# Converting the first 16 weight pieces in pairs (128x1024 operations)

## The chip, the cores and the metric

The kernel runs on one core of one Trainium2 chip. The core has five engines that work side by side, each through its own queue in order: TensorE (PE, matmuls; its weight loads are shown as PEld), VectorE (DVE), ScalarE (ACT), GpSimd (POOL) and SyncE (SP, which here issues most DMAs). The metric is the time of one execution in device microseconds (us). Before the change the median of three runs is 1157.33 us (1157.27 to 1157.82).

## The reference

```python
x = attention(q, k, v)              # 4 batches, 8 heads, 768 positions, 64 each; window 128, 4 sink columns
x = x.transpose(0, 2, 1, 3).reshape(3072, 512)
h = np.maximum(x @ w_in, 0.0)       # w_in (512, 2048)
x = h * h @ w_out                   # w_out (2048, 512), both in float64
e = argmax(x @ w_gate)              # 8 experts, one per token
out = gate_w * eom * (np.maximum(x @ w1[e], 0) @ w2[e])
```

Attention goes into a dense layer pair (w_in, w_out), and that into a layer pair of one expert per token. w_in and w_out arrive as float64. [...]

## The kernel before, in words

The 3072 tokens are 12 blocks (t) of 256. A block goes through attention, in four head pairs (p) of two 128-row pieces, into `xr`; `split_x(t)` then writes `xT`, a high part on ACT and a low part on DVE, in four column groups kk (lines 542 and 543). The dense pair of a block is 16 steps (j): `l1(t, j)` is 12 matmuls of 256 columns (line 576) over the four kk, then a relu on ACT (line 579), a square on DVE or, for odd j of block 0, on POOL (line 580), and the split into high and low `h` (lines 582, 583); `l2(t, j)` is 6 matmuls of 512 columns (line 592). While block t goes through the dense pair, the attention of block t+1 is threaded between its matmuls. The expert stage follows.

The weights are made ready only once, during attention of block 0 and the dense steps of block 0. A *piece* is a slice of w_in (even numbers c) or of w_out (odd c); step j needs pieces 2j and 2j+1, and there are 32. `conv(c)` issues the load of a piece (512 KB) and returns `rest`, which converts it: two ACT operations on the raw words (lines 293, 296), two DVE operations that join the bits in `fbuf` (lines 298, 299), an ACT operation for the high part (line 300) and a DVE operation for the low part (line 301), all 128x512. That is 96 ACT and 96 DVE operations for 32 pieces. `fetch` issues loads two pieces ahead of `cstep`, which converts. Raw pieces lie in three `braw` buffers (the first three) and then in three rotating `stage` buffers; `fbuf` has two halves.

The order of the instructions on each engine is fixed when the program is built: a list scheduler takes, engine by engine, the ready instruction with the highest priority, mostly the earliest in the source. 13 pieces are converted, in source order, ahead of `split_x(0)`, 4 more at step j=0, then two per step. What is ready when, as the scheduler sees it, decides what stands ahead of what. On the chip every engine then follows that list and waits in place.

`xT` has one buffer, so block 1 can be split only when the last `l1` of block 0 has read it. The accumulators of `l1` (`psH`) are two.

Of the kernel before, what the change touches and what calls it, by code (L numbers as in the profile page):

```python
# [8 lines left out]
F32 = mybir.dt.float32  # L9
F32R = mybir.dt.float32r  # L10
BF16 = mybir.dt.bfloat16
I32 = mybir.dt.int32
U32 = mybir.dt.uint32
AF = mybir.ActivationFunctionType
ALU = mybir.AluOpType
# [10 lines left out]
NF = DFF // 128  # L26
# [9 lines left out]

SPLITS = {6: (0, 0), 8: (2, 0), 11: (0, 1), 12: (1, 0), 13: (2, 1), 14: (3, 0)}

NBOOT = 3
NSLOT = NT // 128 + NE - 1  # L40
PRE = 2

# [2 lines left out]
def kern(ctx, tc, q, k, v, n_sink, window, w_in, w_out, w_gate, w_og, w1, w2, out):  # L45
    nc = tc.nc
    V, A, G, PE, SY = nc.vector, nc.scalar, nc.gpsimd, nc.tensor, nc.sync
# [203 lines left out]
    cv = ctx.enter_context(tc.tile_pool(name="cv", bufs=1, side="right"))  # L251
# [15 lines left out]
    WO = [wpool.tile([128, NF // 2, 2, 512], F32R, name="WOa"), None]  # L267
    WIf = WI[:].rearrange("p j a k f -> p (j a k f)")
    WOf = [WO[0][:].rearrange("p j a f -> p (j a f)"), None]

    fbuf = att.tile([128, 2, 512], F32, tag="PT", name="fbuf", bufs=1)

    def conv(c):
        j, which = divmod(c, 2)
        if c < NBOOT:
            raw, dq = braw[c], A
        else:
            raw = cv.tile([128, 512, 2], I32, tag="stage", bufs=3, name="craw")
            dq = SY
        if which == 0:  # L280
            x = dq.dma_start(out=raw[:].rearrange("p (k f) w -> p k (f w)", k=4),
                         in_=w_in.bitcast(I32)[:, 256 * j:256 * j + 256].rearrange("(k p) f -> p k f", p=128))
            hi, lo = (WI[:, j, n].rearrange("p k f -> p (k f)") for n in range(2))
        else:
            x = dq.dma_start(out=raw[:].rearrange("p f w -> p (f w)"), in_=w_out.bitcast(I32)[128 * j:128 * j + 128, :])
            hi, lo = (WO[j // 8][:, j % 8, n] for n in range(2))
        if c < NBOOT:
            tc.keep_in_program_order(x)

        def rest():  # L290
            L, Hh = raw[:, :, 0], raw[:, :, 1]

            x = A.activation(out=Hh.bitcast(F32), in_=Hh.bitcast(F32), func=AF.Copy, scale=2.0 ** -112)
            if c < NBOOT:
                tc.keep_in_program_order(x)
            A.activation(out=L, in_=L.bitcast(U32), func=AF.Copy, scale=0.93 * 2.0 ** -29)
            f, fi = fbuf[:, c % 2], fbuf[:, c % 2].bitcast(I32)
            V.scalar_tensor_tensor(out=fi, in0=Hh, scalar=3, in1=L, op0=ALU.logical_shift_left, op1=ALU.bitwise_or)
            V.scalar_tensor_tensor(out=fi, in0=Hh, scalar=-2147483648, in1=fi, op0=ALU.bitwise_and, op1=ALU.bitwise_or)
            A.activation(out=hi, in_=f, func=AF.Copy)  # L300
            V.tensor_tensor(out=lo, in0=f, in1=hi.bitcast(F32), op=ALU.subtract)
        return rest
# [473 lines left out]
    NC = 2 * NF  # L776
    rests = {}
    st_ = dict(load=0, done=0)

    def fetch(n):  # L780
        while st_["load"] < n:
            rests[st_["load"]] = conv(st_["load"])
            st_["load"] += 1

    def cstep(n):
        for _ in range(n):
            if st_["done"] >= NC:
                return
            fetch(min(NC, st_["done"] + 2))
            rests.pop(st_["done"])()  # L790
            st_["done"] += 1

# [8 lines left out]
            general(gp_)  # L801
    bootS = ExitStack()
    boot = bootS.enter_context(tc.tile_pool(name="boot", bufs=1))
    braw = [boot.tile([128, 512, 2], I32, name=f"braw{n}") for n in range(NBOOT)]
    fetch(NBOOT)
    events = sorted((e for t in range(NBLK) for e in attn_events(t)), key=lambda e: e[0])
    events.reverse()

    def run_to(h):
        while events and events[-1][0] <= h:  # L810
            h_, f = events.pop()
            with (tc.high_priority(200) if h_ < 0 else ExitStack()):
                f()
# [8 lines left out]
    for h in range(-46, 0):  # L822
        run_to(h)
        if h == -38:
            setup2()
        if h >= -39 and h % 3 == 0:
            cstep(1)
    bootS.close()
    wpool2 = ctx.enter_context(tc.tile_pool(name="wpool2", bufs=1))
    WO[1] = wpool2.tile([128, NF // 2, 2, 512], F32R, name="WOb")  # L830
    WOf[1] = WO[1][:].rearrange("p j a f -> p (j a f)")
    split_x(0)

    raw = None

    def load_raw(pc, e, reg=False):

        o = raw[pc]
        if pc < 2:
            a_ = w1[bass.ds(e, 1)] if reg else w1[e:e + 1]  # L840
            SY.dma_start(out=o[:], in_=a_.rearrange("o (k p) f -> p (o k) f", p=128)[:, :, 512 * pc:512 * pc + 512])
        else:
            a_ = w2[bass.ds(e, 1)] if reg else w2[e:e + 1]
            SY.dma_start(out=o[:], in_=a_.rearrange("o (k p) f -> p (o k) f", p=128)[:, 4 * (pc - 2):4 * (pc - 2) + 4, :])
# [103 lines left out]
    for g in range(G2):  # L948
        t, j = divmod(g, NF)
        if t == NBLK - 2 and j == 8:  # L950
            presel()
        if t == NBLK - 1 and j == 0:
            run_to(2 * g - 0.1)
            attS.close()
            m2 = ctx.enter_context(tc.tile_pool(name="m2", bufs=1))
            raw = [m2.tile([128, 4, 512], F32, name=f"raw{pc}") for pc in range(4)]
            pidx = m2.tile([128, NSLOT], I32, name="pidx")
            xgr = [m2.tile([128, XW], F32, name=f"xg{n}")[:] for n in range(PRE)]
            es = [nc.values_load(pre[0:1, n:n + 1], engines=[ET.SP], min_val=0, max_val=NE - 1) for n in range(3)]
            for pc in range(4):  # L960
                load_raw(pc, es[0], True)
            box["base"] = nc.values_load(pre[0:1, 3:4], engines=[ET.SP], min_val=0, max_val=(NE - 1) * REG)
            for s in range(PRE):
                places(s)
                gather(s)
        if t == NBLK - 1 and j in SPLITS:
            pc, half = SPLITS[j]
            split_raw(pc, 4096 * half, True)
            load_raw(pc, es[half + 1], True)
        if t == 0:  # L970
            cstep(max(2 * j + 3, 17 + j) - st_["done"])
        with (tc.high_priority(20) if t == 0 else ExitStack()):
            swap = t > 0 and j == 0
            if swap:
                l2(*divmod(g - 2, NF))
            else:
                l1(t, j)
            run_to(2 * g + 0.9)
            if j == NF - 1 and t + 1 < NBLK:
                split_x(t + 1)  # L980
            if swap:
                l1(t, j)
            elif g >= 2:
                l2(*divmod(g - 2, NF))
            if g >= 2:
                if j == 1 and t > 0:
                    gate_events(t - 1)
            run_to(2 * g + 1.9)
# [149 lines left out]
```

## Time and profile before

| | |
|---|---|
| median of three runs | 1157.33 us |
| the profiled execution | 1156.13 us |
| its span, first to last instruction | 1154.4 us |
| PE, DVE, ACT, POOL busy | 97%, 63%, 56%, 36% |
| mean granted TensorE clock | 0.991 |
| conversion operations, first to last start | 22.8 to 129.5 us |

From about 135 us on PE is busy nearly all the time. The stage of the change is the first 135 us; there DVE and ACT are the busier engines. Each digit of the page's slices is the busy share of 28.9 us, too coarse for this stage, so the rows below are taken from finer views.

### The profile page before, as it was taken

How to read it: one execution, taken by the hardware profiler on the slowest of the kernel's cores; microseconds unless marked ns; L12 is line 12 of the kernel's file. 1: busy time of each engine (PE TensorE's matmuls, PEld its weight loads, DVE VectorE, ACT ScalarE, POOL GpSimd, SP SyncE). 2: the span in 40 equal slices, each digit the busy share in tenths (PEclk: the TensorE clock that was granted, in tenths of full speed). 3: DMA queues.
4: the chain of work that ended last, by engine and by line, in shares of the span. 5: the costliest groups of instructions: out<-in, count | busy, mean ns of one | idle time of the engine just before them, and what ended most of it. 6: DMA issues, size and time to landing. Idle time of an engine off the chain costs nothing. (4 is left out here: it accounts for less than half of the span.)

```text
span 1154.4 us, 23899 instructions
## 1 busy us (share of the span) xinstructions
PE 1118.4 (97%) x7082; PEld 943.0 (82%) x7082; DVE 731.2 (63%) x2039; ACT 642.0 (56%) x1761; POOL 418.4 (36%) x915
## 2 busy tenths in 40 slices
PE   8979999999999999999999999999999999999996
PEld 4657788888888888888888888997788888888884
DVE  4898867676767667676667676567312576763153
ACT  4988776767677767677767676453222222222200
POOL 3123463355564336565326665210211231111111
PEclk8989999999999999999999999999999999999998
DMA  6666211111211111211112110394411455753110
GB/s 156 186 207 182 72 28 50 39 50 37 54 28 49 38 46 36 56 29 43 35 47 47 38 31 1 63 224 153 129 47 46 167 190 191 241 195 119 48 44 24
DMA packets 139611, 100.08 MB, mean 87 GB/s; under 512 B 104127, under 2 KB 112447, under 8 KB 139458
## 3 DMA queue, kind: packets, MB, share of 16 engines
q1 hardware_dynamic: 131618, 82.28, 25.8%
q0 software_dynamic: 5408, 14.19, 3.8%
q10 hardware_dynamic: 2432, 1.84, 0.5%
q8 instruction: 64, 1.05, 0.4%
q14 instruction: 89, 0.73, 0.3%
HBM read 85.56 MB, written 13.76 MB: 86 GB/s over the span
## 5 line engine op out<-in xcount | busy, mean ns | idle before, releaser
L576 PE MATMUL psh<-xT,WI 128*128 128x256 f32 x2304 | 311.6, 284 | 4.2 <-ACT WI L300 2.1
L576 PEld LDWEIGHTS psh<-xT,WI 128*128 128x128 f32 x2304 | 293.6, 189 | 19.6 <-ACT WI L300 3.1
L906 PE MATMUL psh<-WI,xt 128*128 (+1 forms) x672 | 165.1, 399 | 1.0 <-ACT xt L886 0.7
L592 PE MATMUL psx<-WOa,h 128*128 128x512 f32 x576 | 159.0, 410 | 5.2 <-ACT h L582 4.7
L580 DVE TENSOR_TENSOR r<-r 128x256 f32<-128x256 f32 x184 | 85.5, 465 | 116.3 <-ACT r L579 115.2
L592 PE MATMUL psx<-WOb,h 128*128 128x512 f32 x576 | 155.3, 406 | 1.9 <-ACT h L582 1.6
L906 PEld LDWEIGHTS psh<-WI,xt 128*128 128x128 f32 x672 | 123.9, 188 | 29.3 <-ACT xt L886 1.4
L592 PEld LDWEIGHTS psx<-WOa,h 128*128 128x128 f32 x576 | 101.8, 190 | 23.4 <-ACT h L582 5.5
L592 PEld LDWEIGHTS psx<-WOb,h 128*128 128x128 f32 x576 | 101.4, 188 | 21.9 <-ACT h L582 2.9
L439 ACT ACTIVATE P<-P,st 128x260 f32<-128x260 f32 (+1 forms) x192 | 93.8, 489 | 44.5 <-DVE st L436 35.3
L922 DVE TENSOR_TENSOR ht<-psht,ht 128x512 fp32r<-128x512 f32 x56 | 38.5, 689 | 125.1 <-ACT ht L886 124.7
L579 ACT ACTIVATE r<-psh 128x256 f32<-128x256 f32 x192 | 71.7, 373 | 61.6 <-PE psh L576 58.8
L484 POOL TENSOR_SCALAR_AFFINE_SELECT PT<-PT 128x256 fp32r<-128x256 f32 x224 | 98.3, 472 | 17.1 <-DVE PT L480 16.9
L944 POOL DMA_INDIRECT out_dram<-xg,pidx x28 | 30.9, 1103 | 202.4 <-ACT xg L943 160.8
L583 DVE TENSOR_TENSOR h<-r,h 128x256 fp32r<-128x256 f32 x192 | 87.1, 454 | 18.2 <-ACT h L582 12.9
L582 ACT ACTIVATE h<-r 128x256 fp32r<-128x256 f32 x192 | 79.2, 414 | 27.6 <-DVE r L580 23.2
L436 DVE CUSTOM_DVE_ANT_0 P<-pss,M 128x260 f32<-128x260 f32 (+1 forms) x184 | 72.6, 403 | 20.1 <-PE pss L432 9.7
L935 PE MATMUL psy<-WOb,ht 128*128 (+1 forms) x336 | 85.1, 402 | 0.0
L912 ACT ACTIVATE r<-psh 128x512 f32<-128x512 f32 x48 | 28.7, 598 | 101.0 <-PE psh L906 99.1
L935 PE MATMUL psy<-WOa,ht 128*128 (+1 forms) x336 | 84.0, 397 | 0.0
L451 ACT ACTIVATE P<-P,st 128x132 f32<-128x132 f32 (+2 forms) x168 | 62.2, 415 | 34.2 <-DVE st L442 34.1
L935 PEld LDWEIGHTS psy<-WOa,ht 128*128 128x128 f32 x336 | 62.7, 188 | 14.7
(440 smaller groups left out, 1854.9 us busy)
## 6 DMA issues: line engine op xcount, KB each, us to landing
raw<-in_moe_w_dram SPq DMA_DIRECT2D x36, 1024.0 KB, 5.7
craw<-in_moe_w_out_dram SPq DMA_DIRECT2D x15, 512.0 KB, 3.5
craw<-in_moe_w_in_dram SPq DMA_DIRECT2D x14, 512.0 KB, 3.8
x2tab<-x2s SPq DMA_DIRECT2D x24, 256.5 KB, 3.0
kn<-in_k_dram SPq DMA_DIRECT2D x64, 96.0 KB, 2.5
vn<-in_v_dram SPq DMA_DIRECT2D x64, 96.0 KB, 2.2
qn<-in_q_dram SPq DMA_DIRECT2D x92, 64.0 KB, 2.1
kn<-in_k_dram SPq DMA_DIRECT2D x32, 64.0 KB, 1.9
```

Source lines behind the costliest of these rows:

```text
L436: V.tensor_tensor_reduce(out=P[:, e, 0:W], in0=ps[e][:, 0:W], in1=mask[:, 0:W], scale=-SCALE, scalar=3.0e38, op0=ALU.add, op1=ALU.min, acc ...
L439: A.activation(out=P[:, e, 0:W], in_=P[:, e, 0:W], func=AF.Exp, scale=-1.0, bias=st[:, e:e + 1], accum_out=st[:, 4 + e:5 + e])
L451: A.activation(out=P[:, e, 0:W], in_=P[:, e, 0:W], func=AF.Copy, scale=st[:, 6 + e:7 + e])
L484: G.affine_select(out=both[:, 1 - b, e], in_=bf[:, 0, e], pattern=[[0, 2], [1 - 2 * b, 128]], compare_op=ALU.is_gt if b else ALU.is_ge, fi ...
L576: PE.matmul(ps[:], lhsT=WI[:, j, a_, kk, :], rhs=x[:, b_, kk, :], start=(n == 0), stop=(n == 11))
L579: A.activation(out=hq[:], in_=ps[:], func=AF.Relu)
L580: (G if t == 0 and j % 2 else V).tensor_tensor(out=hq[:], in0=hq[:], in1=hq[:], op=ALU.mult)
L582: A.activation(out=o[:, 0], in_=hq[:], func=AF.Copy)
L583: V.tensor_tensor(out=o[:, 1], in0=hq[:], in1=o[:, 0].bitcast(F32), op=ALU.subtract)
L592: PE.matmul(acc[t][m][:], lhsT=o[:, a_, 128 * m:128 * m + 128], rhs=WO[j // 8][:, j % 8, b_, :], start=(j == 0 and n == 0), stop=(j == NF ...
L906: PE.matmul(ps[:], lhsT=o[:, a_, kk, :], rhs=wview(n, par + 2048 * b_ + 512 * kk, 512), start=(c == 0), stop=(c == 11))
L935: PE.matmul(yp[s][:], lhsT=o[:, a_, kk, :], rhs=wview(2 + n, par + 2048 * b_ + 512 * kk, 512), start=(n == 0 and kk == 0 and c == 0), stop ...
```

## The change

For the first 16 pieces (8 pairs: step j's slice of w_in and of w_out) the two raw pieces lie side by side in one `braw` buffer, and the first two ACT and the first two DVE operations of the conversion run once on both, 128x1024, into a `bf` buffer of two slices. The high and the low part stay 128x512 per piece. There are three `braw` buffers of a pair (8 KB per partition each) and two `bf` (4 KB each). These 32 KB are where the last eight slices of the second weights (`WOb`) are put later, so `WOb` is made at step j=0 and not ahead of `split_x(0)`. Loads run up to three pairs ahead (`fetch`) where they ran two pieces ahead; the first four are issued by ACT, the others by SP. Pieces 16 to 31 are converted as before.

```diff
--- before.py
+++ after.py
@@ -36,7 +36,7 @@
 
 SPLITS = {6: (0, 0), 8: (2, 0), 11: (0, 1), 12: (1, 0), 13: (2, 1), 14: (3, 0)}
 
-NBOOT = 3
+NBOOT = 16
 NSLOT = NT // 128 + NE - 1
 PRE = 2
 
@@ -273,30 +273,39 @@
     def conv(c):
         j, which = divmod(c, 2)
         if c < NBOOT:
-            raw, dq = braw[c], A
+            if which == 0:
+                braw[j] = boot.tile([128, 2, 512, 2], I32, tag="pair", bufs=3, name="braw")
+            raw, dq = braw[j][:, which], A if c < 4 else SY
         else:
-            raw = cv.tile([128, 512, 2], I32, tag="stage", bufs=3, name="craw")
+            raw = cv.tile([128, 512, 2], I32, tag="stage", bufs=3, name="craw")[:]
             dq = SY
         if which == 0:
-            x = dq.dma_start(out=raw[:].rearrange("p (k f) w -> p k (f w)", k=4),
+            x = dq.dma_start(out=raw.rearrange("p (k f) w -> p k (f w)", k=4),
                          in_=w_in.bitcast(I32)[:, 256 * j:256 * j + 256].rearrange("(k p) f -> p k f", p=128))
             hi, lo = (WI[:, j, n].rearrange("p k f -> p (k f)") for n in range(2))
         else:
-            x = dq.dma_start(out=raw[:].rearrange("p f w -> p (f w)"), in_=w_out.bitcast(I32)[128 * j:128 * j + 128, :])
+            x = dq.dma_start(out=raw.rearrange("p f w -> p (f w)"), in_=w_out.bitcast(I32)[128 * j:128 * j + 128, :])
             hi, lo = (WO[j // 8][:, j % 8, n] for n in range(2))
-        if c < NBOOT:
+        if c < 4:
             tc.keep_in_program_order(x)
 
         def rest():
-            L, Hh = raw[:, :, 0], raw[:, :, 1]
-
-            x = A.activation(out=Hh.bitcast(F32), in_=Hh.bitcast(F32), func=AF.Copy, scale=2.0 ** -112)
-            if c < NBOOT:
-                tc.keep_in_program_order(x)
-            A.activation(out=L, in_=L.bitcast(U32), func=AF.Copy, scale=0.93 * 2.0 ** -29)
-            f, fi = fbuf[:, c % 2], fbuf[:, c % 2].bitcast(I32)
-            V.scalar_tensor_tensor(out=fi, in0=Hh, scalar=3, in1=L, op0=ALU.logical_shift_left, op1=ALU.bitwise_or)
-            V.scalar_tensor_tensor(out=fi, in0=Hh, scalar=-2147483648, in1=fi, op0=ALU.bitwise_and, op1=ALU.bitwise_or)
+            if c < NBOOT and which == 0:
+                src = braw[j][:].rearrange("p c f w -> p (c f) w")
+                bf[j] = boot.tile([128, 2, 512], F32, tag="bf", bufs=2, name="bf")
+                f_ = bf[j][:].rearrange("p c f -> p (c f)")
+            elif c >= NBOOT:
+                src, f_ = raw, fbuf[:, c % 2]
+            if c >= NBOOT or which == 0:
+                L, Hh, fi = src[:, :, 0], src[:, :, 1], f_.bitcast(I32)
+
+                x = A.activation(out=Hh.bitcast(F32), in_=Hh.bitcast(F32), func=AF.Copy, scale=2.0 ** -112)
+                if c < 4:
+                    tc.keep_in_program_order(x)
+                A.activation(out=L, in_=L.bitcast(U32), func=AF.Copy, scale=0.93 * 2.0 ** -29)
+                V.scalar_tensor_tensor(out=fi, in0=Hh, scalar=3, in1=L, op0=ALU.logical_shift_left, op1=ALU.bitwise_or)
+                V.scalar_tensor_tensor(out=fi, in0=Hh, scalar=-2147483648, in1=fi, op0=ALU.bitwise_and, op1=ALU.bitwise_or)
+            f = bf[j][:, which] if c < NBOOT else f_
             A.activation(out=hi, in_=f, func=AF.Copy)
             V.tensor_tensor(out=lo, in0=f, in1=hi.bitcast(F32), op=ALU.subtract)
         return rest
@@ -786,7 +795,8 @@
         for _ in range(n):
             if st_["done"] >= NC:
                 return
-            fetch(min(NC, st_["done"] + 2))
+            n = st_["done"]
+            fetch(min(NC, max(n + 2, min(NBOOT, n // 2 * 2 + 6))))
             rests.pop(st_["done"])()
             st_["done"] += 1
 
@@ -801,8 +811,8 @@
             general(gp_)
     bootS = ExitStack()
     boot = bootS.enter_context(tc.tile_pool(name="boot", bufs=1))
-    braw = [boot.tile([128, 512, 2], I32, name=f"braw{n}") for n in range(NBOOT)]
-    fetch(NBOOT)
+    braw, bf = {}, {}
+    fetch(4)
     events = sorted((e for t in range(NBLK) for e in attn_events(t)), key=lambda e: e[0])
     events.reverse()
 
@@ -825,10 +835,6 @@
             setup2()
         if h >= -39 and h % 3 == 0:
             cstep(1)
-    bootS.close()
-    wpool2 = ctx.enter_context(tc.tile_pool(name="wpool2", bufs=1))
-    WO[1] = wpool2.tile([128, NF // 2, 2, 512], F32R, name="WOb")
-    WOf[1] = WO[1][:].rearrange("p j a f -> p (j a f)")
     split_x(0)
 
     raw = None
@@ -967,6 +973,12 @@
             pc, half = SPLITS[j]
             split_raw(pc, 4096 * half, True)
             load_raw(pc, es[half + 1], True)
+        if g == 0:
+            cstep(NBOOT - st_["done"])
+            bootS.close()
+            wpool2 = ctx.enter_context(tc.tile_pool(name="wpool2", bufs=1))
+            WO[1] = wpool2.tile([128, NF // 2, 2, 512], F32R, name="WOb")
+            WOf[1] = WO[1][:].rearrange("p j a f -> p (j a f)")
         if t == 0:
             cstep(max(2 * j + 3, 17 + j) - st_["done"])
         with (tc.high_priority(20) if t == 0 else ExitStack()):
```

The change moves instructions on every engine until some way into block 1; from there on the lists are the same. Two places matter here (line numbers of the changed kernel are 9 to 12 higher: 552 is 543, 306 and 307 are 298 and 299, 310 is 301, 585 is 576, 349 is 340, 477 is 468, 511 is 502).

On DVE, around the low parts of `xT` for block 0. Before the change:

```order
L449 TENSOR_SCALAR P<-P,st 128x260 x2
L298 SCALAR_TENSOR_TENSOR fbuf<-craw 128x512
L301 TENSOR_TENSOR WOa<-fbuf,WOa 128x512
L299 SCALAR_TENSOR_TENSOR fbuf<-craw,fbuf 128x512
L298 SCALAR_TENSOR_TENSOR fbuf<-craw 128x512
L543 TENSOR_TENSOR xT<-xr,xT 128x256
L299 SCALAR_TENSOR_TENSOR fbuf<-craw,fbuf 128x512
L301 TENSOR_TENSOR WI<-fbuf,WI 128x512
L543 TENSOR_TENSOR xT<-xr,xT 128x256
L301 TENSOR_TENSOR WOa<-fbuf,WOa 128x512
L543 TENSOR_TENSOR xT<-xr,xT 128x256 x2
```

On the same engine, after the change, the last part of the same stretch:

```order
L307 SCALAR_TENSOR_TENSOR bf<-braw,bf 128x1024
L552 TENSOR_TENSOR xT<-xr,xT 128x256 x3
L306 SCALAR_TENSOR_TENSOR bf<-braw 128x1024
L310 TENSOR_TENSOR WI<-bf,WI 128x512
L310 TENSOR_TENSOR WOa<-bf,WOa 128x512
L307 SCALAR_TENSOR_TENSOR bf<-braw,bf 128x1024
L306 SCALAR_TENSOR_TENSOR bf<-braw 128x1024
L310 TENSOR_TENSOR WI<-bf,WI 128x512
L310 TENSOR_TENSOR WOa<-bf,WOa 128x512
L307 SCALAR_TENSOR_TENSOR bf<-braw,bf 128x1024
L552 TENSOR_TENSOR xT<-xr,xT 128x256
```

Counted from the start of the list, 18 conversion operations of 512 columns stood ahead of the fourth low part of `xT`; now 14 of 1024 and 12 of 512 do. Ahead of the first square (line 580) it was 21 of 512, and is 15 of 1024 and 16 of 512. Ahead of the first relu on ACT (line 579) it was 22 of 512, and is 16 of 1024 and 19 of 512. Ahead of the first low part of `xT` for block 1 it was 96, and is 16 of 1024 and 64 of 512, which is all of them.

On PE, at the start of the dense steps of block 0. Before:

```order
L468 MATMUL pspt<-ident,P 128x128 x4
L576 MATMUL psh<-xT,WI 128x256 x8
L340 MATMUL psk__1291<-ident,kn 128x128 x3
L502 MATMUL pso<-PT_1262,vn 64x128 x2
L576 MATMUL psh<-xT,WI 128x256 x6
L502 MATMUL pso<-PT_1262,vn 64x128 x2
L576 MATMUL psh<-xT,WI 128x256 x10
```

After, with `psk` and `pso` of block 1's attention as above:

```order
L477 MATMUL pspt<-ident,P 128x128 x4
L585 MATMUL psh<-xT,WI 128x256 x35
L349 MATMUL psk__1259<-ident,kn 128x128
L585 MATMUL psh<-xT,WI 128x256 x2
L349 MATMUL psk__1259<-ident,kn 128x128
L585 MATMUL psh<-xT,WI 128x256 x4
```

The attention of block 1 stood between the first `l1` matmuls; now nearly three whole steps stand in one run, with nothing of block 1 between.

## Rows read from the trace of the kernel before

**Rows 1.** Stretches: us, busy of PE, PEld, DVE, ACT, POOL (instructions), clock, DMA share, GB/s.
```profile
26.00:47.00 21.00, 18.77 (x122) 11.20 (x121) 18.57 (x58) 19.43 (x55) 4.69 (x18) 1.00 0.59 149
53.00:130.00 77.00, 65.52 (x384) 50.59 (x383) 70.56 (x159) 65.35 (x152) 23.03 (x42) 0.96 0.63 185
...
130.00:140.00 10.00, 9.89 (x67) 8.17 (x66) 7.99 (x29) 8.36 (x29) 3.77 (x14) 1.00 0.06 15
140.00:150.00 10.00, 9.01 (x65) 7.72 (x64) 6.86 (x20) 7.20 (x21) 8.23 (x21) 1.00 0.18 40
150.00:160.00 10.00, 10.00 (x70) 8.87 (x70) 7.16 (x26) 7.17 (x23) 5.91 (x16) 1.00 0.09 21
```

**Rows 2.** Timeline of DVE: start, duration, line, operation.
```profile
49.85 0.76 DVE L543 TENSOR_TENSOR xT<-xr,xT 128x256 fp32r<-128x256 f32 x2
...
52.90 0.42 DVE L580 TENSOR_TENSOR r<-r 128x256 f32<-128x256 f32 x1
53.23 0.69 DVE L299 SCALAR_TENSOR_TENSOR fbuf<-craw,fbuf 128x512 int32<-128x512 int32 x1
...
73.49 0.68 DVE L301 TENSOR_TENSOR WI<-fbuf,WI 128x512 fp32r<-128x512 f32 x1
74.10 0.68 DVE L299 SCALAR_TENSOR_TENSOR fbuf<-craw,fbuf 128x512 int32<-128x512 int32 x1
74.70 0.41 DVE L436 CUSTOM_DVE_ANT_0 P<-pss,M 128x260 f32<-128x260 f32 x1
...
131.14 1.09 DVE L543 TENSOR_TENSOR xT<-xr,xT 128x256 fp32r<-128x256 f32 x3
```

**Rows 3.** Timeline of ACT.
```profile
48.07 0.62 ACT L472 ACTIVATE PT<-pspt 128x512 f32<-128x512 f32 x1
48.55 0.66 ACT L300 ACTIVATE WOa<-fbuf 128x512 fp32r<-128x512 f32 x1
49.07 0.71 ACT L293 ACTIVATE craw<-craw 128x512 f32<-128x512 f32 x1
49.63 0.71 ACT L296 ACTIVATE craw<-craw 128x512 int32<-128x512 uint32 x1
...
52.17 0.39 ACT L579 ACTIVATE r<-psh 128x256 f32<-128x256 f32 x1
52.45 0.27 ACT L504 ACTIVATE xr<-pso 128x128 f32<-128x128 f32 x1
```

**Rows 4.** Groups by shape, 0 to 130 us: count, busy, mean ns, idle before.
```profile
L298 DVE SCALAR_TENSOR_TENSOR fbuf<-craw 128x512 int32<-128x512 int32 x29 | 20.1, 692 | 2.4 <-ACT craw L296 2.1
L293 ACT ACTIVATE craw<-craw 128x512 f32<-128x512 f32 x29 | 19.7, 681 | 4.4 <-DMA craw<-in_moe_w_in_dram 2.6 <-DMA craw<-in_moe_w_out_dram 1.8
L580 DVE TENSOR_TENSOR r<-r 128x256 f32<-128x256 f32 x8 | 3.3, 416 | 0.0
```

**Rows 5.** Timeline of PE; idle before a row in brackets.
```profile
51.27 1.44 PE L576 MATMUL psh<-xT,WI 128*128 128x256 f32 x10
...
76.20 0.71 PE L428 MATMUL pss<-kT,qT 64*128 64x260 f32 x4
80.49 2.93 PE L592 MATMUL psx<-WOa,h 128*128 128x512 f32 x6 [3.58 <-ACT h L582]
...
94.00 2.36 PE L592 MATMUL psx<-WOa,h 128*128 128x512 f32 x9 [1.15 <-ACT h L582]
...
131.94 1.46 PE L576 MATMUL psh<-xT,WI 128*128 128x256 f32 x11
```

**Rows 6.** Stretches around the idle PE, columns as in rows 1.
```profile
78.00:80.00 2.00, 0.00 (x0) 0.00 (x0) 1.84 (x4) 1.34 (x3) 0.00 (x0) 0.79 0.76 257
80.00:82.00 2.00, 1.51 (x4) 1.22 (x5) 1.83 (x5) 1.96 (x6) 0.00 (x0) 0.50 0.37 93
...
84.00:86.00 2.00, 2.00 (x11) 2.00 (x10) 2.00 (x5) 1.80 (x3) 0.91 (x2) 0.50 0.47 186
86.00:88.00 2.00, 2.00 (x17) 1.92 (x17) 2.00 (x6) 1.36 (x3) 1.58 (x3) 1.00 0.54 148
```

**Rows 7.** The first loads, stretches as in rows 1.
```profile
14.00:16.00 2.00, 2.00 (x10) 1.35 (x9) 1.23 (x8) 1.69 (x6) 0.00 (x0) 0.50 1.05 384
16.00:18.00 2.00, 2.00 (x10) 1.01 (x8) 1.04 (x7) 0.86 (x3) 0.00 (x0) 0.57 1.04 200
...
20.00:22.00 2.00, 2.00 (x16) 1.19 (x16) 1.65 (x8) 1.35 (x6) 0.00 (x0) 1.00 0.93 276
```

## The prediction

> **What bounds the kernel now.** I read the views from coarse to fine. First the stretches [rows 1]: after 150 us PE is busy all the time, so whatever the change does must be read at the moment when block 1's dense steps begin on PE; later lists are the same and can only pass the shift on. From 53 to 130 us, the dense steps of block 0, PE is busy 65.5 of 77 us, DVE 70.6, ACT 65.4. So there DVE is nearest to being full, ACT follows, and PE has 11.5 us of waiting. Then the timelines of the three engines [rows 2, 3, 5], to find three moments: the low part of `xT` is complete for block 0 (the pair of rows at 49.85; the fourth starts near 50.2), PE has done the first two `l1` steps at 51.27+1.44 = 52.7, and the first `l1` of block 1 ends at 131.94+1.46 = 133.4. Last, the stretches around PE's longest wait [rows 6]: after 3.58 us of idleness [rows 5] the granted clock is 0.50 (1.2 GHz) and it is 1.00 again (2.4 GHz) only in the stretch that begins at 86.
>
> **Part 1, fewer instructions.** 64 operations of 512 columns become 32 of 1024: 16 fewer on DVE, 16 fewer on ACT. No row shows 1024 columns, so I bound it. From start to start DVE takes 0.605 us for 512 columns (73.49, 74.10, 74.70) and 0.33 for 256 (52.90 to 53.23) [rows 2], so 256 more columns cost 0.275 and 1024 come to 0.605+0.55 = 1.155, against 1.21 for two. That saves 0.055 a pair, 16 x 0.055 = 0.9 us. By durations instead, 692 and 416 ns [rows 4], it would be 2 x 692 - (692+552) = 140 ns, 2.2 us in all; but a duration overlaps the next start by some 0.08 us, so this is the upper end; the lower is 0 (a 1024 that takes two 512). I take 0.9, since starts are what an engine's queue is made of. On ACT: 0.56 for 512 raw words, 0.52 and 0.28 for 512 and 256 other columns [rows 3], so 1024 come to 0.56+0.48 = 1.04, 0.08 less than two, 1.3 us in all.
>
> The Trainium skill (VectorE: DVE Perf Modes, section "The TRN2 errata") says that such operations pay a fixed cost for each instruction, about 150 cycles, once for a large tile and once for each of many small ones. Its formula gives 691 ns for 512 columns, and the row has 692; by it 16 fewer would save 2.5 us on DVE (an estimate from that page) and the sum below would lose 1.6 us more if DVE were the bound. The starts in rows 2 disagree: between neighbours that don't wait most of this cost is not paid.
>
> **Part 2, what now stands ahead.** Loads now run three pairs ahead, so more conversions are ready early; they come earlier in the source than `split_x(0)`, and the scheduler puts them ahead of it. Ahead of the fourth low part of `xT` DVE has 14 x 1.155 + 12 x 0.605 = 23.4 us of conversion where it had 18 x 0.605 = 10.9, so 12.5 more; ahead of the first square 15 x 1.155 + 16 x 0.605 = 27.0 against 12.7, 14.3 more. Ahead of the first relu ACT has 16 x 1.04 + 19 x 0.54 = 26.9 against 22 x 0.54 = 11.9, 15.0 more (0.54 is the mean of 0.56 and 0.52). Idle time can take little of it: from 26 to 47 us DVE is idle 2.4 of 21 us and ACT 1.6 [rows 1], and the first conversion stands no earlier than before. So `xT` is complete at about 50.2+12.5 = 62.7 and the first relu starts at 52.2+15.0 = 67.2 (both 2.4 earlier at the lower bound). PE is in order and stands from about 45 us in its run of 35 `l1` matmuls, with nothing of block 1 between. The third step must wait for an accumulator, which the first relu frees: 67.5. Where PE had two steps behind it at 52.7 it now has them at 67.5, which is 14.8 us later.
>
> **Part 3, what PE has to give.** From 52.7 to 133.4 PE took 80.7 us. Of that 11.5 was waiting [rows 1], and from 80.49 to 86 it ran 5.5 us at half clock, which lost 2.75 [rows 5, 6]. So its work at full clock without a wait is 80.7-11.5-2.75 = 66.4 us. From 67.5 that ends at 133.9, 0.5 us later than now, if nothing waits. Two things will. The wait from 45 to 62.7 is far longer than the 3.58 us that led to 0.50, so PE restarts at 1.2 GHz; the loss lies between 0 and 2.75, and as part of it falls before 67.5, where PE waits anyway, I take 1.5. And some waits stay: between none and all of today's share (66.4/65.5 x 11.5, some 11.7 us). DVE has 15.2 us less conversion left after its first square (75 x 0.605 before, 1.155 + 48 x 0.605 now), so I take few, 2.0, about two like the one of 1.15 at 94.00 [rows 5]. Against this, PE idles 0.1+1.0 us from 130 to 150 [rows 1], which a later start can swallow: -1.1.
>
> **Edits that cost nothing.** The 0.9 and 1.3 us of part 1 lie on engines that PE no longer waits for; if that cover goes they are the gain of the first rival. `WOb` made later: its first write is still behind the last reader of the buffers in whose place it lies, on the same two engines, so no wait is added beyond their order; if one showed, it would be one operation, 0.6 us. One more load is issued by ACT, before 20 us, where ACT is half idle (1.69 and 0.86 of 2 us in rows 7). On SP the loads of the last three pairs wait until DVE frees a buffer, and loads of k and v for block 1 stand behind them; PE takes those only after its run of 35, so this wait lies beside the one of part 2.
>
> **Sum.** 0.5+1.5+2.0-1.1 = +2.9 us. On the profiled execution (1156.13, with 1.7 us around its span) that is 1159.0; on the median, 1.2 us above it, 1160.2. I give the latter.
>
> **Rivals.** First, DVE sets the end and the change gains. For it: DVE's work up to block 1's `xT` (131.14 [rows 2]) shrinks by 0.9, and of its 6.4 us of waiting from 53 to 130 a part comes from ACT, which in turn waits 4.4 us for raw pieces [rows 4]; deep loads remove that. If none of it goes the gain is 0.9, if half goes 0.9+3.2 = 4.1; I take 3.0, nearer to the second, since the loads are surely earlier: 1154.3. For PE to follow it must start its third step earlier than 67.5 or need some 5 us less than 66.4, which can be if part of what the profile counts as busy PE is waiting in disguise. Against it stands part 2. Chance 0.28. Second, delay and slack cancel: no restart loss and no waits, 0.5-1.1 = -0.6, 1156.7. For it, DVE and ACT have less to do while PE catches up; against it, the clock in rows 6. Chance 0.24. Third, the loads collide. Three pieces, 1.5 MB, move to before 25 us, ahead of q, k, v pieces of block 0, where the DMA share is already 0.93 to 1.05 [rows 7]; at the 200 to 276 GB/s there they take 5.4 to 7.5 us, and attention of block 0, a chain of short waits, would be late by up to that. It decides from the point where DVE has no other work; the time would be 2.9+5.4, some 1165.6. Chance 0.08: DVE has conversions to do meanwhile. The Trainium skill (DMA: Bandwidth & Descriptors, section "Issuing engines are not separate DMA queues") says that DMAs issued by different engines run on the same 16 DMA engines and interleave, so issuing four from ACT would not shield the small loads; rows 7 don't show who was held up.
>
> **Chances.** The forecast has 0.40. A measurement of this kernel can tell some 0.2%, 2.3 us: below 1155.0 is faster, above 1159.6 slower. Faster: most of the first rival and a little of the second, 0.26. Same: most of the second, the low side of the forecast (fewer waits) and the edge of the first, 0.32. Slower: 0.42. The range goes from 1152.5 (the first rival's far end, with 0.1 below) to 1166 (waits of 8 instead of 2, or the collision, with 0.1 above). The forecast's own range is 1158 to 1164.
>
> **What would show it.** In the profile after: low parts of `xT` complete near 60 to 65 us where it was 50; PE idle between 45 and 62 and a clock of 0.50 behind it; the first relu near 67; from 68 to 134 PE with under 4 us of waiting; 1024-column operations 1.16 us apart on DVE. I am wrong if the first relu comes before 62, or if the first `l1` of block 1 ends before 132: then the order matters less than the loads.

## The result, and the profile after

The changed kernel takes 1172.67 us (median of four, 1168.03 to 1179.58) beside 1157.3 for the kernel before on the same chip: ratio 1.0128, 95% interval 1.0101 to 1.0154. Timed once more later (a2_again below): 1169.48 us, ratio 1.0104, interval 1.0089 to 1.0118. So it is 12 to 15 us slower. The forecast was 1160.2, the range up to 1166: the sign was right, the size was not. The profile shown first is that of the longest execution, 1179.58 us with a span of 1177.7; a profile of 1170.39 us is set beside it further down.

The stretches of the changed kernel, with the columns of [rows 1]:

```profile
26.00:47.00 21.00, 16.83 (x88) 9.17 (x88) 11.90 (x38) 14.04 (x38) 6.62 (x16) 0.76 0.56 139
53.00:130.00 77.00, 64.19 (x340) 47.97 (x339) 63.80 (x142) 60.50 (x131) 20.10 (x34) 0.79 0.53 159
130.00:140.00 10.00, 8.39 (x47) 6.61 (x45) 8.14 (x16) 7.08 (x18) 5.65 (x9) 0.83 0.51 146
140.00:150.00 10.00, 10.00 (x63) 7.77 (x64) 8.12 (x20) 6.75 (x20) 3.55 (x10) 1.00 0.23 53
150.00:160.00 10.00, 9.48 (x57) 7.81 (x57) 6.84 (x25) 7.00 (x24) 4.34 (x13) 1.00 0.06 13
```

Before 47 us, where block 0's attention runs, DVE is now busy 11.90 us of 21 (18.57 before), and the clock is 0.76 (1.00). The loss begins there, earlier than where the forecast looked for it.

This is the timeline of DVE in the changed kernel (start, duration, line, operation), with the three moments of [rows 2] and the same part of `xT` for block 2:

```profile
66.99 1.22 DVE L306 SCALAR_TENSOR_TENSOR bf<-braw 128x1024 int32<-128x1024 int32 x1
68.13 0.69 DVE L310 TENSOR_TENSOR WI<-bf,WI 128x512 fp32r<-128x512 f32 x1
...
79.70 0.42 DVE L552 TENSOR_TENSOR xT<-xr,xT 128x256 fp32r<-128x256 f32 x1
...
150.59 1.08 DVE L552 TENSOR_TENSOR xT<-xr,xT 128x256 fp32r<-128x256 f32 x3
...
213.54 0.42 DVE L552 TENSOR_TENSOR xT<-xr,xT 128x256 fp32r<-128x256 f32 x1
```

`xT` is complete for block 0 at 80.1 instead of 50.6, for block 1 it starts 19.5 us later than in [rows 2], for block 2 20.8 later (192.69 before). From there to block 11 the shift stays between 20.8 and 21.0, as the forecast said of the later lists; the expert stage behind them added 2.4 in this execution.

This is ACT's last `xr` of block 0's attention, first in the kernel before:

```profile
42.72 0.28 ACT L504 ACTIVATE xr<-psh 128x128 f32<-128x128 f32 x1 [0.69 <-PE psh L502]
```

and in the changed kernel, with the first relu (52.17 in [rows 3]):

```profile
59.13 0.28 ACT L513 ACTIVATE xr<-psh 128x128 f32<-128x128 f32 x1 [1.64 <-PE psh L511]
...
81.84 0.72 ACT L588 ACTIVATE r<-psh 128x256 f32<-128x256 f32 x2
```

So of the 29.7 us by which the relu is late, 16.4 were lost before the attention ended. PE shows where (idle before a row in brackets):

```profile
38.81 1.24 PE L437 MATMUL psx<-kT,qT 64*128 64x260 f32 x4 [3.46 <-POOL kT L360]
...
70.94 3.93 PE L585 MATMUL psh<-xT,WI 128*128 128x256 f32 x18 [4.48 <-DVE xT L552]
80.17 1.22 PE L585 MATMUL psh<-xT,WI 128*128 128x256 f32 x4 [5.30 <-DVE xT L552]
```

The first row is the new one: these scores waited for a copy of `kT` on POOL. This is POOL in the changed kernel:

```profile
27.03 0.25 POOL L360 COPY kT<-sk 128x4 f32<-128x4 f32 x1
32.94 0.89 POOL L242 CAST w<-tmp 128x64 bf16<-128x64 f32 x1 [5.66 <-DMA tmp<-n_moe_w_output_gate_dram]
33.91 0.31 POOL L243 TENSOR_TENSOR tmp<-tmp,w 128x64 f32<-128x64 f32 x1
34.16 1.38 POOL L360 COPY kT<-sk 128x4 f32<-128x4 f32 x2
35.48 0.23 POOL L244 CAST w<-tmp 128x64 bf16<-128x64 f32 x1
35.79 0.31 POOL L245 TENSOR_TENSOR w<-tmp,w 128x64 bf16<-128x64 f32 x1
36.04 1.18 POOL L356 CAST sk<-kT 128x4 fp32r<-128x4 f32 x1
...
37.51 1.24 POOL L360 COPY kT<-sk 128x4 f32<-128x4 f32 x1
```

Four operations on the gate weights (242 to 245), whose first reader is a matmul at 196.0 us, wait 5.66 us for their load, and the copies of `kT` that the scores wait for stand behind the first of them. This is called the POOL block below. In the kernel before, the first of the four ran without a wait:

```profile
22.99 0.24 POOL L242 CAST w<-tmp 128x64 bf16<-128x64 f32 x1
```

SP shows why, first in the kernel before, then in the changed one:

```profile
20.39 0.39 SPq L238 DMA_DIRECT2D tmp<-in_moe_w_gate_dram  x1
20.82 0.54 SPq L239 DMA_DIRECT2D tmp<-n_moe_w_output_gate_dram  x1
```

```profile
29.83 0.45 SPq L238 DMA_DIRECT2D tmp<-in_moe_w_gate_dram  x1
30.94 0.37 SPq L239 DMA_DIRECT2D tmp<-n_moe_w_output_gate_dram  x1
```

The deep loads and the q, k, v loads that moved with them now stand ahead of these two, which come 9.4 and 10.1 us later.

### The profile page after: what moved, and what is told of

It reads as the page before. It is cut to its first block, busy times and chain, and to the rows that moved or that the text cites. A ratio compares the mean times of both kernels' runs of the same rounds, so it can differ in the third digit from the quotient of the medians.

```text
span 1177.7 us, 23847 instructions
## 1 busy us (share of the span) xinstructions
PE 1137.5 (97%) x7082; PEld 952.3 (81%) x7082; DVE 729.6 (62%) x2023; ACT 640.1 (54%) x1745; POOL 425.4 (36%) x915
## 5 line engine op out<-in xcount | busy, mean ns | idle before, releaser
L585 PE MATMUL psh<-xT,WI 128*128 128x256 f32 x2304 | 317.0, 286 | 12.2 <-DVE xT L552 9.8
L585 PEld LDWEIGHTS psh<-xT,WI 128*128 128x128 f32 x2304 | 297.9, 191 | 28.5 <-DVE xT L552 10.3
L950 POOL DMA_INDIRECT out_dram<-xg,pidx x28 | 28.5, 1019 | 201.0 <-ACT xg L949 159.4
```

The costliest lines, as they stand in the source:

```text
L585: PE.matmul(ps[:], lhsT=WI[:, j, a_, kk, :], rhs=x[:, b_, kk, :], start=(n == 0), stop=(n == 11))
```

## The experiments

There were three theories at first. "Loads": the earlier weight loads delay attention. "Order": conversions ahead of `xT` delay PE's start, as forecast. "Wide operations": 1024 columns hold up the others. After the first four runs came a fourth, "DVE idle": DVE's work up to block 1's `xT` hardly changes, and the end moves by what DVE idles. These are the sums of DVE behind it (busy is the third of the pairs), before and after:

```profile
12.00:131.14 119.14, 104.33 (x615) 74.30 (x616) 102.67 (x270) 100.62 (x254) 31.17 (x78) 0.95 0.65 185
```

```profile
12.00:150.59 138.59, 119.49 (x602) 81.37 (x603) 100.72 (x253) 99.22 (x238) 37.44 (x78) 0.78 0.56 159
```

DVE's busy time fell by 1.95 us, its idle time rose from 16.5 to 37.9. The table gives for every kernel, from one profiled execution: last `xr` of the attention, first relu, DVE's idle time from 12 us to block 1's `xT`, the start of that `xT` (us); and from all its executions the ratio to the kernel before, timed on the same chip, with its 95% interval. The kernel before took 1156.4 to 1161.7 us on the chips used, so times of different experiments are compared by their ratios.

| kernel | last xr | relu | DVE idle | xT of block 1 | ratio |
|---|---|---|---|---|---|
| before | 42.7 | 52.2 | 16.5 | 131.1 | 1 |
| changed | 59.1 | 81.8 | 37.9 | 150.6 | 1.0128 (1.0101-1.0154) |
| a2_again | 52.9 | 75.8 | 29.0 | 141.8 | 1.0104 (1.0089-1.0118) |
| e1_shallow | 49.2 | 71.6 | 27.0 | 138.0 | 1.0070 (1.0052-1.0088) |
| e3_xT_first | 52.8 | 60.2 | 34.1 | 147.0 | 1.0112 (1.0075-1.0149) |
| e5_both | 49.2 | 56.6 | 23.9 | 136.1 | 1.0068 (1.0051-1.0084) |
| e2_deep_512 | 46.7 | 73.1 | 26.0 | 140.4 | 1.0073 (1.0057-1.0090) |
| f1_pairs_from4 | 43.9 | 61.2 | 22.8 | 135.7 | 1.0037 (1.0021-1.0052) |
| f3_from4_xT | 43.1 | 48.7 | 21.9 | 133.1 | 1.0054 (1.0030-1.0078) |
| f2_before_xT | 43.3 | 47.9 | 22.0 | 135.3 | 1.0045 (1.0031-1.0060) |
| d1_more_dve | 42.2 | 51.7 | 20.0 | 138.9 | 1.0083 (1.0068-1.0098) |
| g1_w3_late | 49.9 | 72.1 | 25.1 | 137.9 | 1.0061 (1.0042-1.0081) |
| g2_deep_from4 | 47.5 | 64.9 | 26.8 | 140.0 | 1.0048 (1.0028-1.0069) |
| g3_w3_from4 | 47.5 | 64.4 | 24.2 | 137.7 | 1.0064 (1.0051-1.0078) |
| h0_three_512 | 44.7 | 72.0 | 25.7 | 140.1 | 1.0083 (1.0061-1.0104) |
| h1_three_from4 | 44.7 | 58.6 | 21.1 | 133.1 | 1.0018 (1.0003-1.0034) |
| h2_three_from4_xT | 44.7 | 51.3 | 25.6 | 140.7 | 1.0067 (1.0052-1.0082) |
| h4_three_from8_xT | 43.9 | 51.8 | 20.4 | 134.1 | 1.0015 (1.0006-1.0023) |

**e1_shallow**

```diff
-            fetch(min(NC, max(n + 2, min(NBOOT, n // 2 * 2 + 6))))
+            fetch(min(NC, n + 2))
```

> The changed kernel with its loads two pieces ahead again (pairs, buffers and the late WOb stay; on DVE the conversions still stand ahead of xT as in the changed kernel, 14 of 1024 columns and 12 of 512). Theory 'loads': the extra 1 MB ahead of q, k, v and of the gate weights made the attention of block 0 late; here its last xr is back near 43 us (59 in the changed kernel, 42.7 before), PE keeps full clock from 37 to 60 us, the first relu comes near 67 as the prediction had it, and the time is 1158 to 1162 us. Theory 'order': only the place of the conversions counts; the first relu stays near 80 us and the time near 1170. Theory 'wide operations' (1024 columns hold up POOL and the chain): attention stays late, PE idles near 35 us again, time near 1170.

Measured: 1165.46 us beside 1156.35, ratio 1.0070. With shallow loads 3 to 6 thousandths of the 10 to 13 are gone: attention ends 10 us earlier than in the changed kernel's longest profile, and the clock is 1.00 from 26 to 54 us. But the first `xr` stays at 24.3 (19.0 before), so the attention is not back at 43, and the time is outside what "loads" gave.

**e3_xT_first and e5_both** (the second has e1's edit too)

```diff
-    split_x(0)
+    with tc.high_priority(400):
+        split_x(0)
```

> The changed kernel with the xT parts of block 0 at high priority, so that on DVE only 6 conversions of 1024 and 4 of 512 stand ahead of them (14 and 12 in the changed kernel); loads stay deep. Theory 'order': xT complete and first relu go back by some 12 us or more, time 1157 to 1160. Theory 'loads': attention of block 0 still ends near 59 us with PE at half clock from 37 us on; xT is complete near 64, the first relu near 66 instead of 82, and the time 1162 to 1168. If PE's later work were the bound and not its start, the time would stay at 1168 to 1175.

> Both edits: loads two pieces ahead and xT of block 0 at high priority, the pairs stay. Theory 'loads' and theory 'order' together: attention of block 0 ends near 43 us, xT is complete near 48, the first relu near 50, the time 1154 to 1158. Theory 'wide operations': still above 1162, since the 1024-column operations are all there.

Measured: 1172.05 and 1163.81 us. Neither is where "loads" or "order" had it; e3_xT_first is in the range for a bound in later work, e5_both where "wide operations" had it, which e2_deep_512 tests below. For these kernels "order" falls: from e1_shallow to e5_both the first relu comes 15.1 us earlier and the ratio goes from 1.0070 to 1.0068. The row of PE in e5_both says where the 15 us went:

```profile
67.32 3.20 PE L601 MATMUL psx<-WOa,h 128*128 128x512 f32 x6 [5.62 <-ACT h L591]
```

PE starts early and then waits for ACT, which is busy with conversions until then (from 58.39 to 66.9, almost without a gap).

**e2_deep_512**

```diff
-                src = braw[j][:].rearrange("p c f w -> p (c f) w")
...
-            if c >= NBOOT or which == 0:
-                L, Hh, fi = src[:, :, 0], src[:, :, 1], f_.bitcast(I32)
...
+                f_ = bf[j][:, which]
...
+            L, Hh, fi = raw[:, :, 0], raw[:, :, 1], f_.bitcast(I32)
```

> The changed kernel with its loads deep and its buffers and WOb as they are, but every conversion in 512 columns as before the change. Theories 'loads' and 'order': the width is not what costs, the attention of block 0 still ends past 52 us with PE at half clock and the time stays above 1165. Theory 'wide operations': attention ends near 43 us and the time is 1156 to 1160.

Measured: 1165.84 us, ratio 1.0073 without a single wide operation, where "wide operations" gave 1156 to 1160. The width by itself is not what costs: g1_w3_late below has every wide operation and is at 1.0061. That the ratio is 3 to 6 thousandths better than the changed kernel's goes with another difference: here the four gate operations stand behind the copies of `kT` (the first runs at 37.84), so there is no POOL block. The attention ended at 46.7, not past 52 as expected; the wait sits at a load of q:

```profile
30.74 0.30 PE L379 MATMUL psq<-ident,qn 128*128 128x128 f32 x1 [3.18 <-DMA qn<-in_q_dram]
```

**f1_pairs_from4 and f3_from4_xT** (e1's loads, pairs from piece 4 on; the second with `xT` at high priority)

```diff
+            one = c < 4
...
+            elif one:
+                src, f_ = raw, bf[j][:, which]
...
-            if c >= NBOOT or which == 0:
+            if c >= NBOOT or one or which == 0:
```

> Loads two pieces ahead as in e1_shallow, and pairs only from the fifth piece on; the first four pieces are converted in 512 columns, which leaves the order of PE up to about 20 us as it was before the change. Theory 'DVE idle' (DVE's work up to block 1's xT is nearly the same in all kernels, about 100 us, and the end moves by the time that DVE idles in the attention of block 0): first xr back at 19 us (24.3 in e1_shallow), last xr near 43, DVE idle from 12 us to block 1's xT 16 to 19 us, time 1155 to 1159. Theory 'order' (first relu sets the end): conversions still stand ahead of xT, first relu near 60, time 1160 to 1165. Theory 'wide operations': 12 of the 16 are left, time 1162 to 1165.

> f1_pairs_from4 with xT of block 0 at high priority. Theory 'DVE idle': as f1_pairs_from4 within 2 us, though the first relu comes some 10 us earlier. Theory 'order': 5 us or more faster than f1_pairs_from4.

Measured: 1162.43 and 1161.38 us beside 1158.03. The attention is back (first `xr` at 18.6 and 17.5), and f3 is no better than f1 with a relu 12.5 us earlier; but DVE idles 22 to 23 us, not 16 to 19, and 4 to 6 us of loss remain, more than "DVE idle" gave.

**f2_before_xT** (the kernel before, with e3's edit)

> The kernel before with xT of block 0 at high priority: 11 conversions stand ahead of it on DVE instead of 18, up to there the order is the same. Theory 'order': first relu some 4 us earlier than 52.2, time 1153 to 1154. Theory 'DVE idle': first relu earlier, block 1's xT where it was (131 to 132 us), time 1156 to 1158.

Measured: 1162.96 us. The relu comes 4.3 us earlier, and the kernel is 5 us slower. Both theories missed the size, and "order" has the wrong sign.

**d1_more_dve** (the kernel before)

```diff
-            V.tensor_tensor(out=lo, in0=f, in1=hi.bitcast(F32), op=ALU.subtract)
+            for _ in range(2 if 20 <= c < 28 else 1):
+                V.tensor_tensor(out=lo, in0=f, in1=hi.bitcast(F32), op=ALU.subtract)
```

> The kernel before with the last DVE operation of the conversion (the low part, 128x512) done twice for pieces 20 to 27: eight more operations of 0.605 us in block 0, 4.8 us of DVE work and nothing else. Theory 'DVE idle' (DVE is the bound of block 0): block 1's xT and the end come 3.5 to 5 us later, 1160 to 1162. If PE with its 11.5 us of waiting is the bound, as the forecast counted: 0 to 1.5 us later.

Measured: 1166.96 us beside 1158.03, 8 to 11 us more for 4.8 us of work, which is more than "DVE idle" gave. Nothing covers DVE's work in block 0; up to block 1's `xT` DVE is busy 4.3 us more, and it idles 3.5 us more, which a full DVE alone doesn't explain. PE's 11.5 us of waiting in [rows 1] is no slack. Whether ACT, nearly as busy there, bounds the block as well is not shown: no run adds work to ACT alone.

**g1_w3_late**

```diff
+        def w3split():
...
+            x = G.tensor_copy(out=part[0], in_=wg[0])
+            tc.add_manual_dep(x.ins, vdone[0].ins.name, mybir.DependencyInfo(mybir.DependencyClass.Sync, mybir.DependencyReason.DATA), reason="later")
```

> The changed kernel with one thing moved: the four small GpSimd operations on the gate weights (w3) wait for vsk instead of standing ahead of the copies of kT; every other engine's order is the same. Theory 'GpSimd behind the gate weights': in the changed kernel its 5.7 us wait for their load held the kT copy, PE stood idle 3.5 us at 35 us and ran at half clock until 86. Here that idle time is gone, the clock stays 1.00 from 37 to 60 us, the last xr comes near 50 instead of 59, DVE idles 8 to 12 us less, time 1160 to 1165. Theory 'loads' without it (q, k, v late by themselves): within 3 us of the changed kernel.

Measured: 1168.87 us beside 1161.72, ratio 1.0061. PE's idle time before the same scores is 0.42 us, the clock is 1.00 from 38 to 50 (the second row shows the first 4 us, with the columns of [rows 1]), the last `xr` comes at 49.9:

```profile
37.00 0.71 PE L443 MATMUL psx<-kT,qT 64*128 64x260 f32 x4 [0.42 <-POOL kT L363]
...
38.00:42.00 4.00, 3.20 (x24) 1.91 (x24) 3.29 (x12) 3.58 (x12) 0.48 (x2) 1.00 0.86 214
```

DVE idles 12.8 us less than in the changed kernel's longest profile and 3.9 less than in a2_again. Moving four small POOL operations, with every other queue's order unchanged, takes away 4 to 7 thousandths of the ratio, two fifths to one half of the loss.

**a2_again** (the changed kernel, not edited)

> The changed kernel once more, nothing edited. Theory 'clock': its times spread over some 10 us again, and a profile with a shorter time shows fewer stretches at 0.50 between 37 and 86 us with the same order and the same 5.7 us wait of GpSimd. Theory 'order alone': times within 1 us of each other, as for the kernel before.

Measured: 1166.44 to 1170.39 us, a spread of 4 us where it was 11.5, so that part of the expectation missed; the shorter time does go with less half clock. POOL waited 5.04 us for the gate weights, 5.66 in the first profile. These are the stretches of the changed kernel's first profile, then those of this one with PE's row at the same scores:

```profile
38.00:42.00 4.00, 3.19 (x10) 1.29 (x10) 0.91 (x2) 0.38 (x1) 1.06 (x3) 0.50 0.50 137
42.00:46.00 4.00, 3.53 (x19) 2.10 (x17) 1.33 (x6) 2.69 (x7) 0.00 (x0) 0.50 0.00 0
50.00:60.00 10.00, 9.31 (x27) 4.50 (x26) 4.99 (x16) 5.12 (x14) 0.78 (x5) 0.50 0.38 138
60.00:70.00 10.00, 5.44 (x21) 2.95 (x20) 8.57 (x14) 9.29 (x16) 6.33 (x1) 0.50 0.80 235
```

```profile
38.64 1.00 PE L437 MATMUL psx<-kT,qT 64*128 64x260 f32 x4 [2.00 <-POOL kT L360]
...
38.00:42.00 4.00, 3.36 (x11) 1.21 (x12) 2.13 (x6) 0.88 (x4) 0.99 (x4) 0.62 0.91 213
42.00:46.00 4.00, 3.30 (x24) 2.07 (x24) 2.36 (x7) 4.00 (x12) 0.00 (x0) 0.96 0.16 36
50.00:60.00 10.00, 6.00 (x35) 3.39 (x35) 9.02 (x22) 9.73 (x18) 3.84 (x4) 0.97 0.73 223
60.00:70.00 10.00, 4.21 (x18) 3.92 (x18) 8.46 (x13) 8.19 (x13) 5.84 (x3) 0.50 0.91 312
```

The same order of instructions went two ways. PE idled 3.46 us in the first and 2.00 in the second before the same scores. The first ran at 0.50 from 38 us past 70 us, and from 50 to 60 PE is busy 9.31 of 10 us with slow matmuls while DVE and ACT are busy only 4.99 and 5.12. The second fell to 0.50 for 3 to 4 us near 40 and ran those 10 us at 0.97; it was at 0.50 from 60 to 80, but there PE had little to do (4.21 of 10 us). Block 1's `xT` differs by 8.8 us. The scores start at 38.81, 38.64 and, in g1_w3_late, 37.00, but the last `xr` comes at 59.1, 52.9 and 49.9. So the wait itself moves the scores by less than 2 us, and most of what the block costs comes behind it. That this is the half clock is the likely reading of three profiles; no run holds the rest fixed and changes the clock alone.

**g2_deep_from4 and g3_w3_from4** (deep loads with pairs from piece 4 on; the second with g1's edit too)

> The changed kernel with deep loads, and pairs only from the fifth piece on. Theory 'two causes that add' (deep loads, and pairs at the start that change PE's order before 20 us): first xr near 19 us, PE waits some 3 us for a q load near 28 as in e2_deep_512, last xr near 47, time 1163 to 1167, that is 1 to 4 us above f1_pairs_from4 and 6 to 9 below the changed kernel. If pairs at the start cost nothing: 1170 or more.

> g1_w3_late with the first four pieces converted in 512 columns: deep loads stay, the GpSimd block and the pairs at the start are gone. If these two are the causes: ratio to before 1.002 to 1.004, like f1_pairs_from4 and h1_three_from4. If deep loads cost by themselves (a q load behind a weight load, as in e2_deep_512): 1.005 to 1.007, no better than g2_deep_from4 and g1_w3_late.

Measured: 1167.66 beside 1161.72, and 1164.95 beside 1156.98. The two causes do not add up: g3 is no faster than g1 or g2, as its second case had it. In g2 itself the four gate operations already run behind the copies of `kT` (at 37.28, without a wait), so its edit had removed the POOL block too and g3 had nothing left to remove. Both wait for q as e2_deep_512 does (2.06 us in g2, 2.62 in g3, at 29.9 and 30.0): the deep loads seem to have a second price, which shows once PE is early enough to meet it. f1, which is g2 without them, is at 1.0037, but its interval overlaps that of g2.

**h0_three_512, h1_three_from4, h2_three_from4_xT, h4_three_from8_xT** (three pieces up front, then two ahead, as before the change; `one` is true for all, for c < 4, c < 4 and c < 8; the last two with `xT` at high priority)

```diff
-            raw, dq = braw[j][:, which], A if c < 4 else SY
+            raw, dq = braw[j][:, which], A if c < 3 else SY
...
-    fetch(4)
+    fetch(3)
```

> As h1_three_from4 without any pair: only the buffers and the place of WOb differ from the kernel before, and with them the order of the conversions (38 of 512 columns stand ahead of xT on DVE, 18 before). The forecast put this edit at nothing, 0.6 us at most: 1156 to 1159. Theory 'order': with 20 more conversions ahead of xT, 12 us, it would be 1163 or more.

> Loads as before the change (three pieces up front on ACT's queue, then two ahead), pairs from the fifth piece on, buffers and WOb as in the changed kernel. Theory 'DVE idle': attention of block 0 ends near 43 us as before; DVE has some 1.5 to 2 us less to do; time 1154 to 1158, the best of the kernels with pairs. If pairs cost something wherever they are: 1159 or more.

> h1_three_from4 with xT of block 0 at high priority (10 conversions of 512 columns ahead of it instead of 14 and 4 of 1024). From e1_shallow to e5_both and from f1_pairs_from4 to f3_from4_xT the same edit gave about 1 us: ratio 1.000 to 1.002. A gain over the kernel before (below 0.998) only if PE has no idle time over 3 us in block 0.

> The same with pairs only from the ninth piece on, so four pairs. Half of the saving on DVE is given up. Theory 'pairs cost where the attention of block 0 runs': 0.998 to 1.001. Theory 'buffers and late WOb cost by themselves' (h0_three_512): 1.002 to 1.006.

Measured: ratios 1.0083, 1.0018, 1.0067, 1.0015. h0 has no pair and no deep load, and loses 10 us: 38 conversions go ahead of `xT` (18 before), and PE stands idle 11.91 us for it:

```profile
66.51 4.64 PE L589 MATMUL psh<-xT,WI 128*128 128x256 f32 x22 [11.91 <-DVE xT L556]
```

That is the size "order" gave for h0. It is not shown to be the cause: no run puts `xT` first in this kernel, and where the same edit was made (e5, f3, h2) it gained nothing. h2 was expected at 1.000 to 1.002 and missed; h4 lies between its two theories. h1 and h4 are the best kernels with pairs. Neither beats the kernel before.

## Why the prediction was wrong, point by point

**What bounds the kernel.** This step failed. I read PE's start as what sets block 1 and took PE's 66.4 us from its third step as the cost of the rest. From first relu to block 1's `xT` it is 79.0 us before, 68.8 in the changed kernel, 66.4 in e1_shallow, 79.6 in e5_both and 86.9 in e3_xT_first: no constant (the forecast's 66.4 ends at another moment, so the likeness of one figure is chance). d1_more_dve shows that DVE, which the first rival named, has no slack; e5_both and f2_before_xT show that an earlier relu gives nothing. So the right sign was luck in part: the delay that the forecast counted, conversions ahead of `xT`, is worth nothing between e1_shallow and e5_both.

**Part 1.** This was right in size and had no weight. Measured start to start: DVE 1.14 us (66.99 to 68.13), forecast 1.155; ACT 1.04 (33.61 to 34.65), as forecast. That is 0.07 a pair on DVE, 1.1 us in all; DVE's busy time up to block 1's `xT` fell by 1.95, with 17 operations fewer. The Trainium skill (VectorE: DVE Perf Modes, section "The TRN2 errata") led to an estimate of 2.5; the measured starts are nearer to the forecast's 0.9.

**Part 2.** This was half right. From the DVE operation that writes `vsk` late in the attention (49.00, 37.48 before) to the fourth low part of `xT` it took 30.7 us, where it was 12.7: 18 us more, and 12.5 were forecast for conversions. But all of it was counted from an attention that I took as unmoved, and that ended 16.4 us later. The sum has no term for that.

**Part 3.** The waits, forecast at 2.0, were indeed few (0.35, 0.34 and 1.26 us from 90 to 149 us), and it did not help. The restart, forecast at 1.5 as a part of what 5.5 us at half clock cost, was too small: the clock was 0.50 for most of 38 to 86 us (0.54 in the mean, 0.93 before).

**Edits that cost nothing.** This is the step that failed most. I followed SP's loads to DVE's buffers and to PE, never to POOL, though the gate loads moved on the queue that I was reading. g1_w3_late prices that at 4 to 7 thousandths, 5 to 8 us, where the sum had nothing. `WOb` made later was put at nothing, 0.6 at most: h0_three_512, which has the buffers, the late `WOb` and their order alone, is 1.0083.

**Rivals.** The first named the bound that d1_more_dve bears out and drew the wrong sign from it: DVE's work fell, but its idle time rose by 21 us. The third, the collision at 0.08, was nearest, with 1165.6; it was priced as a delay of q, k and v, and dismissed since "DVE has conversions to do meanwhile". In the attention DVE stood with its queue at scores that waited for PE, and conversions behind them could not pass. In the changed kernel's first profile:

```profile
43.56 0.43 DVE L445 CUSTOM_DVE_ANT_0 P<-psx,M 128x260 f32<-128x260 f32 x1 [4.65 <-PE pspt L477]
...
45.93 0.69 DVE L310 TENSOR_TENSOR WI<-bf,WI 128x512 fp32r<-128x512 f32 x1
```

**What would show it.** Neither sign of being wrong came (a first relu before 62, block 1's first `l1` done before 132): the relu came at 81.8. Both signs looked for an earlier start, and none for one later than forecast.

**What stays open.** With the POOL block gone (g1, e1) 6 to 7 thousandths remain, so the cause of half the loss is not shown. Two edits did not take them away: without pairs (e2, h0) and without early pairs (g3) they are there too. f1, h1 and h4, whose attention ends before 45 us with a full clock, are at 1.0015 to 1.0037, but h0 and h2 end it as early and lose 1.0083 and 1.0067 behind it. Small changes of order cost several us each here (f2 5 us); what decides among them was not settled.

## What to carry to other kernels

When a load moves on a queue, follow every load behind it to its reader, on every engine, and ask what stands behind that reader in its queue; a small operation that nobody needs soon can hold the chain. Where one engine is full up to some point, add up its idle time there: an earlier start of another engine gives nothing if the full one has as much to do. Look at the granted clock behind a stall as well as at the stall: here one of 3.46 us was followed by half clock for most of 48 us, one of 2.00 by a dip of 3 to 4 us. A kernel whose own times spread may be one in which that differs from execution to execution.

## What the runs showed of the hardware

A POOL operation can take many times its usual time while DVE runs conversions back to back. These rows show the same 128x8 cast twice in the changed kernel, each with the cast that follows it:

```profile
56.75 0.19 POOL L463 CAST psk<-P 128x8 fp32r<-128x8 f32 x1 [2.52 <-DVE P L458]
56.88 0.19 POOL L464 CAST psk<-P 128x8 fp32r<-128x8 f32 x1
...
63.66 7.94 POOL L463 CAST psk<-P 128x8 fp32r<-128x8 f32 x1 [6.44 <-DVE P L458]
71.55 1.21 POOL L464 CAST psk<-P 128x8 fp32r<-128x8 f32 x1
```

The profile's spans on POOL are rough, but the starts say the same: 0.13 us from the first cast to the next one, 7.89 from the second. From 63.52 to 71.5 DVE had no gap; from 56.7 to 58.15 it was idle. In e2_deep_512, with 512 columns, such a cast took 7.20 us, so it is not the width. The Trainium skill (SBUF — State Buffer, section "SBUF: two separate sides") says that DVE and GpSimd share a port pair as an exclusive lock, which a DVE operation with two inputs in SBUF holds against a GpSimd operation that reads SBUF; these conversions are such, and the rows agree, but they show POOL held up over eleven DVE operations in a row (eight conversions and three low parts of `xT`), not one. That the lock is the cause is not tested by a run of its own. The `kT` copies at 34.16 and 37.51 (1.38 us for two and 1.24 for one, where 0.31 and 0.25 are usual) lie beside a DVE that was busy 3.98 of 4 us, and lengthened the block; how much of it, no run separates.
